# A linear-attention block with an MLP behind it on one Trainium2 core: half-width matmul blocks gathered, and the loads of four batches put in another order

## The chip, the core and the metric

The kernel runs on one NeuronCore of a Trainium2 chip. Its engines are TensorE (matmul, PE in the profile, its weight loads PEld), VectorE (DVE), ScalarE (ACT), GpSimd (POOL) and SyncE (SP); SP and POOL are used here to issue DMAs. Each engine works through its own instructions in the order in which the program emits them. The metric is the device time of one execution in microseconds (us), lower is better; a measurement is the median of several executions.

## What is computed

```python
# q, k, v: 8 batches x 8 heads x 576 positions x 64
kv  = einsum('bhsd,bhse->bhde', k, v)          # 64 x 64 per head
out = einsum('bhsd,bhde->bhse', q, kv)
out = out / sqrt(mean(out*out, -1) + 1e-6) * g_norm
x   = out.transpose(0, 2, 1, 3).reshape(8, 576, 512)
xn  = (x - mean(x)) / sqrt(var(x) + 1e-6) * g_ln
y   = x + relu(xn @ w_ch1) @ w_ch2             # 512 -> 2048 -> 512
```

The result is float32, 8 x 576 x 512. Matmuls run in bfloat16.

## The kernel before

**Tiling.** Of the 576 positions of a batch, 512 make four main tiles of 128 rows, and 64 are left. The 64 rows of two batches make one remainder tile, so batches 1, 3, 5 and 7 each close one (called remainder 1, 3, 5, 7). Four remainder tiles form a ninth block, "rem", which the MLP handles last.

**Stages of a batch b.** (1) q, k and v are loaded by POOL's DMA queue, six transfers (`load`, two for each tensor), float32 in HBM to bfloat16, into one of two sets of buffers (b % 2). (2) `kv_of(b)`, L238 to L250: 40 matmuls with 128 rows and 64 columns of weights (128*64 in the profile), pairs of which go to the lower and the upper half of the output partitions; then two ScalarE copies into `kv_pack`. (3) `turn_q_dma(b)`, L201 to L207: VectorE copies q into another order (L203), then SyncE issues a DMA that transposes it (L205) into `qt`. (4) For each tile a `plan_tile`, L371 to L396, with four steps: `first` makes o = q kv on TensorE (L271; a main tile has 4 matmuls of 128*128, a remainder tile 8 of 128*64), its square on ScalarE (L277) and the sum over each head on VectorE (L298); `second` makes the root (ScalarE L308, VectorE L315) and the normed x (VectorE L303, L322, L326, L332); `third` the variance (ScalarE L340); `fourth` the transpose of the normed rows, for batches 2 and up by a DMA on SyncE's queue (L352), into `xT_blk`. The o of a tile sits in one of two PSUM buffers from `first` to `second`. (5) The MLP: `mm1` (L413, ReLU on ScalarE L416) and `mm2` (L429), whose result VectorE combines with x (`finish`, L434) and SyncE stores by two DMAs (L447, L448). "Tile (3,0)" is tile 0 of batch 3.

**What sets the order.** The MLP's matmuls of all batches run one batch after the other. They are cut into ticks: a tick is four or eight matmuls of L413, or four of L429, and every batch has 32 ticks, 16 of `mm1` and 16 of `mm2`; batch b's begin at tick 32 b. An agenda, filled by hand with `at(slot, function)`, holds all other work: at the start of a tick its functions are emitted, sorted by their fractional slot, and each engine receives its part of them in that order. `finish` of a tile is emitted behind the tile's last L429, before the next tick. So the work of batches 2 to 7 up to `xT_blk` lies between the MLP matmuls of earlier batches. In this order, before: `kv_of(3)` at tick 56 and its q at 56.7, remainder 1 at 62 (second step at 64, turn at 69), main tiles of batch 3 at 66, 71, 76, 81, remainder 3 at 82, `kv_of(4)` at 84 and its q at 84.7, main tiles of batch 4 from 96; `kv_of(5)` at 115; remainder 5 at 146, `kv_of(6)` at 147, `kv_of(7)` at 179, remainder 7 at 210.

**Loads.** `load_batch` first copies one element on POOL for each of its arguments (a gate, L98): POOL's queue goes on only when what that element belongs to has arrived. Loads of batch b are gated by the transposed q of batch b-1, those of batch 4 also by the last transpose of batch 2's `xT_blk`. They are issued k, v, q at ticks 47 (batch 3), 68, 100, 132 and 164.

Of the kernel before, what the change touches and what calls it, by code (L numbers as in the profile page):

```python
# [14 lines left out]
def kernel(  # L15
# [11 lines left out]
    nc = tc.nc  # L27
    f32 = mybir.dt.float32
# [5 lines left out]
    B, H, S, D = q.shape  # L34
# [3 lines left out]
    nK = Dm // 128  # L38
    nDe = Dh // 128
    HP = H // 2  # L40
# [3 lines left out]
    J, JJ, JP = 4, 5, 9  # L44
    S_LO = 64 * JJ
    EPS = 1e-6
    NB = 2
# [8 lines left out]
    ps_m = ctx.enter_context(tc.psum_pool(name="ps_m", bufs=1))  # L56
# [15 lines left out]
    q_in = [consts.tile([128, H, JJ, D], bf16, name=f"q_in{i}") for i in range(NB)]  # L72
    k_in = [consts.tile([128, H, JJ, D], bf16, name=f"k_in{i}") for i in range(NB)]
    v_in = [consts.tile([128, H, JJ, D], bf16, name=f"v_in{i}") for i in range(NB)]
    kv_g = consts.tile([128, HP, 128], bf16)
    kv_pack = [consts.tile([128, HP, 128], bf16, name=f"kv_pack{i}") for i in range(4)]
# [9 lines left out]
    def lo(t, b, h0=0, h1=H):  # L86
        return t[b, h0:h1, :S_LO, :].rearrange("h (p j) d -> p h j d", j=JJ)

    def up(t, b, h0=0, h1=H):
        return t[b, h0:h1, S_LO:, :].rearrange("h (p j) d -> p h j d", j=J)  # L90

    def load(dst, t, b, h0=0, h1=H):
        nc.gpsimd.dma_start(dst[:64, h0:h1], lo(t, b, h0, h1))
        nc.gpsimd.dma_start(dst[64:, h0:h1, :J], up(t, b, h0, h1))

    def load_batch(b, *after):
        for element in after:
            nc.gpsimd.tensor_copy(gate, element)  # L98
        load(k_in[b % NB], k, b)
        load(v_in[b % NB], v, b)  # L100
        load(q_in[b % NB], q, b)

    def load_w1(c):
        n = Dh // 4
# [60 lines left out]
    qts, held, blks, rstds, m1s, q_ps = {}, {}, {}, {}, {}, {}  # L165
# [35 lines left out]
    def turn_q_dma(b):  # L201
        q_p = kv_in.tile([128, JJ, H, D], bf16, tag="qp", bufs=2)
        nc.vector.tensor_copy(q_p.rearrange("p j h d -> p h j d"), q_in[b % NB])  # L203
        q_t = qt_pool.tile([128, JJ, HP, 128], bf16, tag="qt", name="qt")
        nc.sync.dma_start_transpose(  # L205
            q_t.rearrange("p j hp t -> p (j hp) t"), q_p.rearrange("p j h d -> p (j h d)"))
        qts[b] = q_t  # L207
# [28 lines left out]
            nc.vector.tensor_mul(kv_g[D:, self.hps, D:], self.odd[D:], g[D:])  # L236
            del self.even, self.odd

    def kv_of(b):
        kv_ps = ps_m.tile([128, HP, D], f32, tag="misc", name="kv_ps")  # L240
        kvp = held[b] = kv_pack[b % 4]
        for hp in range(HP):
            for j in range(JJ):
                for hh in range(2):
                    h = 2 * hp + hh
                    nc.tensor.matmul(kv_ps[hh * D:hh * D + D, hp, :],  # L246
                                     lhsT=k_in[b % NB][:, h, j, :], rhs=v_in[b % NB][:, h, j, :],
                                     start=(j == 0), stop=(j == JJ - 1))
        nc.scalar.copy(kvp[:D, :, :D], kv_ps[:D])  # L249
        nc.scalar.copy(kvp[D:, :, D:], kv_ps[D:])  # L250

    def new_block(n, bufs):
        x_blk = xpool.tile([128, 4, Dm], f32, tag=f"x{n}", bufs=bufs, name="x_blk")
        st_blk = xpool.tile([128, 3, 4], f32, tag=f"st{n}", bufs=bufs, name="st_blk")
        xT_blk = xpool.tile([128, nK, 512], bf16, tag=f"xT{n}", bufs=bufs, name="xT_blk")
        return x_blk, st_blk, xT_blk
# [98 lines left out]
    def main_tile(b, j, pool=None, tag="ops"):  # L355
        q_t, kvp = qts[b], held[b]
        if b not in blks:
            blks[b] = new_block("main", 3)
        return Tile([(slice(0, 128), lambda hp: q_t[:, j, hp, :], kvp)], blks[b], j, pool, tag)

    def rem_tile(b):
        mms = []
        for half, bb in enumerate((b - 1, b)):
            qt, kp = qts.pop(bb), held.pop(bb)
            mms.append((slice(half * 64, (half + 1) * 64),
                        lambda hp, qt=qt: qt[:, J, hp, :64], kp))
        if "rem" not in blks:
            blks["rem"] = new_block("rem", 1)
        return Tile(mms, blks["rem"], b // 2)

    def plan_tile(s, make, turn_at, on_pe):  # L371
        box = []

        def first():
            t = make()
            box.append(t)
            t.o()
            t.sq()
            t.red()

        def second():
            t = box[0]
            t.y()
            t.x()
            t.xc()

        def third():
            box[0].var()

        def fourth():  # L390
            box[0].turn(on_pe)

        at(s, first)
        at(s + 2, second)
        at(s + 6, third)
        at(turn_at, fourth)  # L396

    def m1_of(b):
# [20 lines left out]
    def rstd_of(b):  # L419
        rstd = work.tile([128, 4], f32, tag="rstd", bufs=3, name="rstd")  # L420
        nc.scalar.activation(rstd, blks[b][1][:, 2, :], func=AF.Sqrt, scale=1.0 / Dm, bias=eps_sb)  # L421
        nc.vector.reciprocal(rstd, rstd)  # L422
        rstds[b] = rstd
# [45 lines left out]
    def at(slot, fn):  # L469
        agenda.setdefault(int(slot), []).append((slot, fn))  # L470
# [119 lines left out]
    def next_loads():  # L590
        nc.gpsimd.memset(k_in[0][64:, :, J], 0.0)
        nc.gpsimd.memset(v_in[0][64:, :, J], 0.0)
        load_batch(2)

    at(1, before_1)
    at(2, before_2)
    at(5, lambda: t[2].turn(True))
    at(5.1, before_5)
    at(9.5, next_loads)
    at(11, lambda: t[3].turn(True))  # L600
    for i in range(4):
# [17 lines left out]
    at(14.5, q_start)  # L619
    at(19, q_turns)  # L620
    at(22, lambda: kv_of(1))
    for j, s, tn in ((0, 24, 30), (1, 27, 34), (2, 31, 38), (3, 35, 42)):
        plan_tile(s, lambda j=j: main_tile(1, j), tn, True)
    at(46, lambda: rstd_of(1))

    at(36, lambda: kv_of(2))
    at(36.9, lambda: turn_q_dma(2))
    for j, s, tn in ((0, 45, 51), (1, 49, 55), (2, 53, 61), (3, 57.5, 64)):
        plan_tile(s, lambda j=j: main_tile(2, j), tn, False)
    plan_tile(62, lambda: rem_tile(1), 69, False)  # L630
    at(78, lambda: rstd_of(2))

    for b in range(3, B):
        s = 32 * b
        at(47 if b == 3 else s - 60,
           lambda b=b: load_batch(b, qts[b - 1][:1, J, HP - 1, 127:],
                                  *([blks[2][2][:1, nK - 1, 511:]] if b == 4 else [])))
        d = -41 if b == 3 else -45
        at(s + d + (1 if b < 5 else 0), lambda b=b: kv_of(b))
        at(s + d + 1.7, lambda b=b: turn_q_dma(b))  # L640
        for j in range(J):
            o = s + d + (11 if b == 3 else 13) + 5 * j
            plan_tile(o, lambda b=b, j=j: main_tile(b, j), o + 6, False)
        if b % 2:
            plan_tile(s - 14, lambda b=b: rem_tile(b), s - 8, False)
        at(s + 14, lambda b=b: rstd_of(b))
    at(32 * B + 14, lambda: rstd_of("rem"))


# [56 lines left out]
```

## Time and profile before

| | us |
|---|---|
| median of 5 executions | 290.61 (290.37 to 291.26) |
| the profiled execution | 290.71 |
| span in its profile, first to last instruction | 288.9 |
| TensorE busy | 281.5 |
| VectorE busy | 149.8 |
| ScalarE busy | 153.3 |
| POOL busy | 40.9 |
| L429, 560 matmuls of 128x512 | 125.5 |
| L413, all forms, 1024 | 131.6 |
| L246 (kv), 280 matmuls | 5.8 |
| L271 (o tiles), 156 matmuls | 13.7 |

TensorE's clock was granted at 0.999 of full speed. How to read the rows that follow in the prediction: a row of the timeline gives the start (us from the span's start), the length, engine, source line, operation, output<-inputs, weight tile as rows*columns, shape, and the number of instructions of one kind merged into the row; in brackets stands idle time before it, and what ended it. Matmuls overlap: the length of one runs to its modelled end and is longer than the distance to the next start, so the prediction works with distances between starts. For DMA issues the profile gives the time from issue to landing.

### The profile page before, as it was taken

What the parts mean: (1) busy time and instruction counts of PE and PEld (TensorE: products, weight loads), DVE (VectorE), ACT (ScalarE), POOL (GpSimd) and SP (SyncE); (2) the same over time, 40 slices, a digit from 0 to 9 for tenths busy, and PEclk for the clock granted to TensorE, in tenths of its full rate; (3) what the DMA queues carried; (4) which work ended last, traced back from release to release, by engine and by line L of the source; (5) the groups of instructions that cost most, each with busy time, mean ns of one, the idle gap of its engine ahead of it and who ended that gap; (6) DMA issues with size and microseconds to landing.
All of it is one profiled execution on the core that took longest, in us unless ns stands there. A gap on an engine that the chain in (4) does not pass through costs nothing.

```text
span 288.9 us, 5753 instructions
## 1 busy us (share of the span) xinstructions
PE 281.5 (97%) x2295; PEld 158.0 (55%) x2295; DVE 149.8 (52%) x331; ACT 153.3 (53%) x333; POOL 40.9 (14%) x69
## 2 busy tenths in 40 slices
PE   8889999999999999999999999999999999999994
PEld 3579746995479644444444444444444444444444
DVE  5774119938897783764376935762578200220022
ACT  3577844985379733872288318921893066016400
POOL 8522510041005004100500032000000000000000
PEclk9999999999999999999999999999999999999999
DMA  7999999879786969997995189947202410230033
GB/s 214 199 206 204 201 188 195 209 113 196 139 171 101 194 108 158 201 154 126 153 217 74 39 150 224 151 84 150 56 18 63 102 36 0 47 81 19 0 73 75
DMA packets 67546, 36.76 MB, mean 127 GB/s; under 512 B 35516, under 2 KB 62524, under 8 KB 67520
## 3 DMA queue, kind: packets, MB, share of 16 engines
q0 software_dynamic: 28528, 17.76, 44.8%
q1 hardware_dynamic: 38480, 17.91, 30.8%
q10 hardware_dynamic: 512, 0.72, 0.8%
q8 instruction: 18, 0.29, 0.4%
q14 instruction: 8, 0.07, 0.1%
HBM read 36.71 MB, written 9.44 MB: 160 GB/s over the span
## 4 chain that ended last, share of the span: by engine, by line
PE 84%; DVE 5%; DMA 5%; ACT 2%; issue 1%; SPq 1%; DVEq 0%; POOLq 0%
PE p L413 41%; PE p L429 37%; DMA v_in<-in_v_dram 2%; PE o_ps L271 2%; DMA qt<-q_p 2%; PE kv_ps L246 2%; DMA xT_blk<-xc 1%; DVE ss L298 1%; ACT m L416 1%; DVE x_blk L322 1%; DVE y L303 1%; DVE o_sb L434 1%; ACT rms L308 1%; SPq L205 1%; DVE x_blk L289 0%
## 5 line engine op out<-in xcount | busy, mean ns | idle before, releaser
L413 PE MATMUL p<-xT_blk,w_sb 128*128 128x128 bf16 (+2 forms) x1024 | 131.6, 286 | 0.7 <-DMA xT_blk<-xc 0.3
L429 PE MATMUL p<-w_sb,m 128*128 128x512 bf16 (+2 forms) x608 | 129.1, 368 | 0.0
L416 ACT ACTIVATE m<-p 128x512 bf16<-128x512 f32 x144 | 85.2, 596 | 43.0 <-PE p L413 40.5
L413 PEld LDWEIGHTS <-w_sb 128*128 128x128 bf16 x1024 | 78.7, 98 | 44.9 <-issue 1.6
L429 PEld LDWEIGHTS <-m 128*128 128x128 bf16 x608 | 56.9, 98 | 62.0
L434 DVE SCALAR_TENSOR_TENSOR o_sb<-p,rstd,x_blk 128x512 f32<-128x512 f32 (+2 forms) x38 | 27.3, 720 | 52.2 <-PE p L429 46.6
L277 ACT ACTIVATE sq<-o_ps 128x512 f32<-128x512 f32 x35 | 20.9, 596 | 41.7 <-PE o_ps L271 41.7
L298 DVE TENSOR_REDUCE ss<-sq 128x8 f32<-128x512 f32 x35 | 23.7, 678 | 13.1 <-ACT sq L277 13.0
L340 ACT ACTIVATE dev<-x_blk,st_blk 128x512 f32<-128x512 f32 x36 | 25.7, 714 | 6.2 <-DVE st_blk L326 6.1
L332 DVE SCALAR_TENSOR_TENSOR xc<-x_blk,st_blk,g_ln_sb 128x512 bf16<-128x512 f32 x34 | 25.6, 752 | 1.2
L303 DVE TENSOR_TENSOR y<-o_ps,inv 128x512 f32<-128x512 f32 x33 | 22.8, 692 | 3.4 <-PE p L413 0.5
L322 DVE SCALAR_TENSOR_TENSOR x_blk<-y,g_norm_sb 128x512 f32<-128x512 f32 x33 | 22.8, 692 | 1.1
L315 DVE RECIPROCAL inv<-rms 128x8 f32<-128x8 f32 x36 | 7.2, 201 | 23.1 <-ACT rms L308 23.1
L422 DVE RECIPROCAL rstd<-rstd 128x4 f32<-128x4 f32 x9 | 1.6, 175 | 31.1 <-ACT rstd L421 31.0
L308 ACT ACTIVATE rms<-ss,eps_sb 128x8 f32<-128x8 f32 x36 | 10.7, 296 | 11.6 <-DVE ss L298 11.5
L98 POOL COPY gate<-qt 1x1 bf16<-1x1 bf16 x5 | 0.9, 177 | 106.3 <-DMA qt<-q_p 106.3
L271 PEld LDWEIGHTS <-qt 128*128 128x128 bf16 (+1 forms) x156 | 10.2, 100 | 8.1 <-issue 1.7
L271 PE MATMUL o_ps<-kv_pack,qt 128*128 128x128 bf16 (+1 forms) x156 | 13.7, 220 | 0.1
L198 PE MATMUL p<-fill_sb 128*128 128x512 bf16 x27 | 8.5, 468 | 1.2 <-DVE eps_sb L137 1.2
L340 ACT ACTIVATION_READ_ACCUMULATOR dev<-x_blk,st_blk 128x1 f32 x36 | 6.8, 189 | 0.0
L249 ACT CAST kv_pack<-kv_ps 64x256 bf16<-64x256 f32 x7 | 2.6, 366 | 7.9 <-PE kv_ps L246 7.9
L246 PEld LDWEIGHTS <-k_in 128*64 128x64 bf16 x280 | 5.0, 112 | 2.9 <-issue 2.8
(80 smaller groups left out, 110.6 us busy)
## 6 DMA issues: line engine op xcount, KB each, us to landing
out_dram<-o_sb SPq DMA_DIRECT2D x70, 128.0 KB, 2.5
w_sb<-in_moe_w_ch_dram POOLq DMA_DIRECT2D x8, 512.0 KB, 15.3
q_in<-in_q_dram POOLq DMA_DIRECT2D x7, 320.0 KB, 12.4
k_in<-in_k_dram POOLq DMA_DIRECT2D x7, 320.0 KB, 6.2
v_in<-in_v_dram POOLq DMA_DIRECT2D x7, 320.0 KB, 9.0
q_in<-in_q_dram POOLq DMA_DIRECT2D x8, 256.0 KB, 12.6
k_in<-in_k_dram POOLq DMA_DIRECT2D x7, 256.0 KB, 7.2
v_in<-in_v_dram POOLq DMA_DIRECT2D x7, 256.0 KB, 9.9
```

What stands on the lines that cost most here:

```text
L271: nc.tensor.matmul(flat[rows, hp * 128:(hp + 1) * 128], lhsT=lhsT_of(hp), rhs=kvp[:, hp, :], start=True, stop=True)
L277: nc.scalar.activation(self.sq_t, self.o_ps, func=AF.Square)
L298: nc.vector.tensor_reduce(self.ss, self.sq_t, axis=AX.X, op=ALU.add)
L303: nc.vector.tensor_mul(self.y_t, self.o_ps, self.inv().to_broadcast([128, H, D]))
L308: nc.scalar.activation(self.r, self.ss, func=AF.Sqrt, scale=1.0 / D, bias=eps_sb)
L322: nc.vector.scalar_tensor_tensor(x_blk[:, ts].rearrange("p (h d) -> p h d", h=H), in0=self.y_t, scalar=1.0, in1=g_norm_sb.to_broadcast([12 ...
L332: nc.vector.scalar_tensor_tensor(self.xc_t, in0=x_blk[:, self.ts], scalar=st[:, 1, self.ts:self.ts + 1], in1=g_ln_sb, op0=ALU.add, op1=ALU ...
L340: nc.scalar.activation(dev, x_blk[:, ts], func=AF.Square, bias=st[:, 1, ts:ts + 1], accum_out=st[:, 2, ts:ts + 1])
L413: nc.tensor.matmul(p1[:, i, :], lhsT=w1_sb[:, kk, de * 128:(de + 1) * 128], rhs=blk[2][:, kk, sl], start=(kk == 0), stop=(kk == nK - 1))
L416: nc.scalar.activation(m1[:, de0:de0 + per, sl], p1, func=AF.Relu)
L429: nc.tensor.matmul(p2[:, c0:c1], lhsT=m1s[b][:, de, ts * 128:(ts + 1) * 128], rhs=w2_sb[:, de, c0:c1], start=(de == 0), stop=(de == nDe - 1))
L434: nc.vector.scalar_tensor_tensor(o_sb[:, c0:c1], in0=p2[:, c0:c1], scalar=rstds[b][:, ts:ts + 1], in1=blks[b][0][:, ts, c0:c1], op0=ALU.mu ...
```

## The change

`kv_of` takes one or more batches, computes them in one PSUM tile and copies them afterwards. Remainder tiles 1, 3 and 5 are emitted directly behind a kv block: remainder 1 behind kv 3 at tick 56.1 (its second step stays at 64, its turn at 69), remainder 3 behind kv 4 at 87.1 (kv 4 moves from 84 to 87, the second step is at 90, the turn at 96), remainder 5 behind kv 6 and kv 7, which are computed together at tick 152 (second step 154, turn 160). Remainder 7 and kv 5 stay. Main tiles of batch 3 stand at 66, 70.5, 75 and 79.5, those of batch 4 at 97, 101.75, 106.5 and 111.25; q of batch 4 is turned at 85.6. The loads of batch 4 are in the order q, k, v. Those of batch 6 are q, k, v, and k and v of batch 7 follow them at tick 132; q of batch 7 comes alone at 164. The gates are the same, but for k and v of batch 7, which are now behind the gate of batch 6.

```diff
-    def load_batch(b, *after):
+    def load_batches(what, *after):
         for element in after:
             nc.gpsimd.tensor_copy(gate, element)
-        load(k_in[b % NB], k, b)
-        load(v_in[b % NB], v, b)
-        load(q_in[b % NB], q, b)
+        tensors = {"k": (k_in, k), "v": (v_in, v), "q": (q_in, q)}
+        for name, b in what:
+            dst, src = tensors[name]
+            load(dst[b % NB], src, b)
...
-    def kv_of(b):
-        kv_ps = ps_m.tile([128, HP, D], f32, tag="misc", name="kv_ps")
-        kvp = held[b] = kv_pack[b % 4]
...
+    def kv_of(*bs):
+        kv_ps = ps_m.tile([128, len(bs), HP, D], f32, tag="misc", name="kv_ps")
+        for i, b in enumerate(bs):
+            for hp in range(HP):
+                for j in range(JJ):
+                    for hh in range(2):
+                        h = 2 * hp + hh
+                        nc.tensor.matmul(
+                            kv_ps[hh * D:hh * D + D, i, hp, :], lhsT=k_in[b % NB][:, h, j, :],
+                            rhs=v_in[b % NB][:, h, j, :], start=(j == 0), stop=(j == JJ - 1))
+        for i, b in enumerate(bs):
+            kvp = held[b] = kv_pack[b % 4]
+            nc.scalar.copy(kvp[:D, :, :D], kv_ps[:D, i])
+            nc.scalar.copy(kvp[D:, :, D:], kv_ps[D:, i])
...
-    def plan_tile(s, make, turn_at, on_pe):
+    def plan_tile(s, make, turn_at, on_pe, x_at=None):
...
-        at(s + 2, second)
-        at(s + 6, third)
+        at(x_at or s + 2, second)
+        at((x_at or s + 2) + 4, third)
...
-    plan_tile(62, lambda: rem_tile(1), 69, False)
...
-    for b in range(3, B):
-        s = 32 * b
-        at(47 if b == 3 else s - 60,
-           lambda b=b: load_batch(b, qts[b - 1][:1, J, HP - 1, 127:],
-                                  *([blks[2][2][:1, nK - 1, 511:]] if b == 4 else [])))
-        d = -41 if b == 3 else -45
-        at(s + d + (1 if b < 5 else 0), lambda b=b: kv_of(b))
-        at(s + d + 1.7, lambda b=b: turn_q_dma(b))
+    def turned_q(b):
+        return qts[b][:1, J, HP - 1, 127:]
+    at(47, lambda: load_batches((("k", 3), ("v", 3), ("q", 3)), turned_q(2)))
+    at(68, lambda: load_batches((("q", 4), ("k", 4), ("v", 4)),
+                                turned_q(3), blks[2][2][:1, nK - 1, 511:]))
+    at(100, lambda: load_batches((("k", 5), ("v", 5), ("q", 5)), turned_q(4)))
+    at(132, lambda: load_batches((("q", 6), ("k", 6), ("v", 6), ("k", 7), ("v", 7)),
+                                 turned_q(5)))
+    at(164, lambda: load_batches((("q", 7),), turned_q(6)))
+    at(115, lambda: kv_of(5))
+    for s, bs, rem, x_at, tn in ((56, (3,), 1, 64, 69), (87, (4,), 3, 90, 96),
+                                 (152, (6, 7), 5, 154, 160)):
+        at(s, lambda bs=bs: kv_of(*bs))
+        plan_tile(s + .1, lambda rem=rem: rem_tile(rem), tn, False, x_at)
+    plan_tile(210, lambda: rem_tile(7), 216, False)
+    for b, at_q, at_o, step in ((3, 56.7, 66, 4.5), (4, 85.6, 97, 4.75),
+                                *((b, 32 * b - 43.3, 32 * b - 32, 5) for b in range(5, B))):
+        at(at_q, lambda b=b: turn_q_dma(b))
         for j in range(J):
-            o = s + d + (11 if b == 3 else 13) + 5 * j
+            o = at_o + step * j
             plan_tile(o, lambda b=b, j=j: main_tile(b, j), o + 6, False)
-        if b % 2:
-            plan_tile(s - 14, lambda b=b: rem_tile(b), s - 8, False)
-        at(s + 14, lambda b=b: rstd_of(b))
+        at(32 * b + 14, lambda b=b: rstd_of(b))
```

More of the change, by code (lines that the diff above doesn't have):

```diff
@@ L237, in times_g @@
             del self.even, self.odd
-    def kv_of(b):
-        kv_ps = ps_m.tile([128, HP, D], f32, tag="misc", name="kv_ps")
-        kvp = held[b] = kv_pack[b % 4]
[L242 to L250, printed above, removed]
+    def kv_of(*bs):
[12 more added lines that the diff above has]
+            nc.scalar.copy(kvp[D:, :, D:], kv_ps[D:, i])
     def new_block(n, bufs):
@@ L592, in next_loads @@
         nc.gpsimd.memset(v_in[0][64:, :, J], 0.0)
-        load_batch(2)
+        load_batches((("k", 2), ("v", 2), ("q", 2)))
     at(1, before_1)
```

## The prediction

> **What bounds the kernel now.** I read the page first, then TensorE's row in the timeline (its waits list says nearly nothing), then VectorE, SyncE's queue and the POOL queue over 72 to 112 us.
>
> ```profile
> span 288.9 us, 5753 instructions
> PE 281.5 (97%) x2295; PEld 158.0 (55%) x2295; DVE 149.8 (52%) x331; ACT 153.3 (53%) x333; POOL 40.9 (14%) x69
> PE 84%; DVE 5%; DMA 5%; ACT 2%; issue 1%; SPq 1%; DVEq 0%; POOLq 0%
> ```
>
> TensorE has work in 97% of the span and is 84% of the chain that ended last. From 18 us on, a change is worth what it takes from TensorE's row: the pauses around the small-tile blocks, and the few stalls. TensorE's timeline around batch 5's blocks:
>
> ```profile
> 156.23 1.89 PE L429 MATMUL p<-w_sb,m 128*128 128x512 bf16 x8
> 158.05 0.41 PE L271 MATMUL o_ps<-kv_pack,qt 128*64 128x128 bf16 x8
> 158.40 1.04 PE L429 MATMUL p<-w_sb,m 128*128 128x512 bf16 x4
> 159.37 0.82 PE L246 MATMUL kv_ps<-v_in,k_in 128*64 128x64 bf16 x40
> 160.12 5.14 PE L429 MATMUL p<-w_sb,m 128*128 128x512 bf16 x23
> ```
>
> L429's pitch is 0.216 us (52 from 130.29 to 141.53). Eight from 156.23 end at 157.96; the remainder tile (128*64, half-width) starts at 158.05, and the next L429 at 158.40: 0.45 us with the 0.01 that the first L429 loses. Its work is 4 pairs that run side by side at about 0.055: 0.22. So 0.23 us is entry and exit. The kv block occupies 159.27 to 160.13, 0.86 us; its pairs have a pitch of 0.032 (19 pitches between its first and last start), 20 pairs make 0.63, and 0.23 is left again. An ordinary o tile (128*128) between L413s costs only its 0.22. **Price of one excursion into half-width tiling: 0.23 us**; there are eleven (kv 1 to 7, remainders 1, 3, 5, 7).
>
> The stalls: VectorE and SyncE bring q of batches 3 and 4 late.
>
> ```profile
> 81.24 1.91 PE L413 MATMUL p<-xT_blk,w_sb 128*128 128x256 bf16 x16
> 83.20 0.40 PE L271 MATMUL o_ps<-kv_pack,qt 128*128 128x128 bf16 x4
> ...
> 101.08 10.53 PE L429 MATMUL p<-w_sb,m 128*128 128x512 bf16 x48
> 111.69 0.40 PE L271 MATMUL o_ps<-kv_pack,qt 128*128 128x128 bf16 x4
> 112.37 4.48 PE L413 MATMUL p<-xT_blk,w_sb 128*128 128x512 bf16 x20 [0.29 <-DMA xT_blk<-xc]
> ```
>
> L413's 256-wide pitch is 0.109 (40 from 83.44 to 87.80), so 16 from 81.24 end at 82.99: tile (3,0) waited 0.21 for q 3's transpose (landed 83.16). 48 L429 from 101.08 end at 111.46: tile (4,0) waited 0.23 for q 4. Its four matmuls end at 111.91; L413 starts at 112.37, 0.46 late, for xT of tile (3,3), whose transpose stands behind q 4's on SyncE's queue.
>
> **Part 1, excursions.** kv 3 with remainder 1, kv 4 with remainder 3, and kv 6, kv 7 and remainder 5 become three blocks instead of seven: eleven become seven. Four times 0.23 is 0.92 less. That kv and remainder matmuls need no pause between each other no trace of before shows; both are 128*64. Bounds: all 0.92, or 0.23 only (kv 6 to kv 7, the same form). I take 0.92, since the rows give the same price to both forms.
>
> A rule puts this higher: the Trainium skill, "TensorE: Matmul & The Clock Gate", Single matmul latency, gives a lone matmul a fixed part of about 166 ns beyond its streaming at full clock. Two such drains would make an excursion 0.33 by estimate, and the sum 1.3 instead of 0.92; the rows above say 0.23, and they decide.
>
> **Part 2, q of batch 3 (worse).** Remainder 1's o, Square and reduction move from tick 62 to 56.1, ahead of the copy q_p at 56.7. VectorE runs without idle there:
>
> ```profile
> 76.20 0.74 DVE L434 SCALAR_TENSOR_TENSOR o_sb<-p,rstd,x_blk 128x512 f32<-128x512 f32 x1
> 76.86 0.82 DVE L203 COPY q_p<-q_in 128x2560 bf16<-128x2560 bf16 x1
> 77.60 0.68 DVE L298 TENSOR_REDUCE ss<-sq 128x8 f32<-128x512 f32 x1
> ```
>
> The added reduction (pitch 0.60) puts q_p at 77.46 to 78.28. SyncE's queue was busy with stores until 78.08 and began q 3's transpose at 78.18, so only 0.16 of the 0.60 reaches it: 78.34, landing 4.98 later at 83.32, tile (3,0) at 83.36. TensorE arrives there 0.23 earlier, at 82.76, and waits 0.60 instead of 0.21. So at this point the new kernel is 0.16 behind, the first excursion's gain already spent. ScalarE's added Square ends about 75.1, before its reader's turn. The o buffers cost nothing: tile (2,3) needs the one that y of (2,2) frees at 74.58, and TensorE comes at 74.76; the remainder's buffer is held to tick 64, and tile (3,0) can take the other.
>
> The same 0.60 goes down VectorE and SyncE: stores of batch 1 (82.04) and xT of (2,2) and (2,3) (83.19, 85.81) issue 0.60 later. xT of (2,3) landed about 88.42 (the gate below starts on it at 88.48), then 89.02; L413 needs it at tick 72, which TensorE now reaches at 83.36 + two o tiles of 0.22 + six ticks of 0.873 (eight L413) = 89.04. I put 0.05 there, about the gate's distance from the landing; a late transpose makes it 0.3.
>
> **Part 3, loads of batch 4.** They start when that xT has landed.
>
> ```profile
> 88.48 0.18 POOL L98 COPY gate<-xT_blk 1x1 bf16<-1x1 bf16 x1 [5.03 <-DMA xT_blk<-xc]
> 89.67 0.68 POOL L93 DMA_DIRECT2D k_in<-in_k_dram  x1 [1.00 <-PE p L413]
> ```
>
> The listing of DMA issues, asked for each one's stretch, gives landings at 94.9, 96.6 (k), 98.3, 100.0 (v), 101.9 and 103.1 (q): the last 13.4 after the first issue. The order q, k, v gives q these first places and v the last. The first issue comes 1.19 after the gate's start here, but 0.48 to 0.52 after it in batches 3, 5, 6 and 7; the gate at 89.08 therefore gives 89.6 to 90.3. I take 89.67, the time of before and next to what those four rows give, and v at 103.1 plus 0.3, because the store of batch 2's first tile moves from 103.31 to about 101.8 (VectorE no longer has remainder 3's chain before it) and meets the last load: 103.4. Bounds for the last landing from the other batches: 13.2 after the first issue (batch 3) and 15.6 (batch 6), 102.9 to 105.9.
>
> The 1.00 us has a page: the Trainium skill, "SBUF — State Buffer", SBUF: two separate sides, says that VectorE and GpSimd lock a shared port pair against each other, so that POOL cannot write descriptors meanwhile. VectorE's xc ran from 88.86 to 89.61 here. If that was the cause, the issue stays at 89.67 although the gate is later; without the rule it could be 90.3 and the sum 0.6 higher. No run here isolates it.
>
> TensorE reaches kv 4 (tick 87) so: 83.36, plus 12.91 (before: 83.20 to 96.11), plus 0.22 for tile (3,3), now before tick 80, plus 28 times 0.216 = 6.05: 102.54, with the 0.05 above 102.59. v lands 103.4, so **kv 4 waits about 0.85**; bounds 0.3 and 3.3, and nothing if the issue comes half a microsecond earlier. Queued behind it on TensorE is everything. This is the term that I am least sure of.
>
> In return q 4 lands at 96.6, its copy stands at tick 85.6 without remainder 3's chain ahead (about 101.7 instead of 105.75), and xT of (3,3) precedes it on SyncE: both waits at 111 to 112 go, 0.23 + 0.46 = 0.69. What is late next there, q 4's transpose, lands about 109, some 3 us early.
>
> **Part 4, batches 6 and 7.** Ten loads instead of six follow the gate, whose time moves with TensorE. Six took 15.6 from the first issue. Four more are 1.18 MB; at 196 GB/s (the rate of the stretch 95 to 98 us) 6.0, with a transpose's share some 6.6: 22.2. Tick 152 was at 164.46; without remainder 5 (0.45) and kv 6 (0.86) it is at 163.15, 24.0 after the old first issue at 139.12. Slack 1.8, so I cost it at nothing. The far end is batch 5's pace (six in 18.3, with three tiles' stores among them) for all ten: 30.5, a wait of 6.5; the stores lie in batch 6's 15.6 already, so this end is left in the tenth above the range. kv 7 leaves tick 179, q 7 alone follows later, and nothing waits for it.
>
> **The sum**, against the profiled run's 290.71 (span 288.9 plus 1.8 around it): excursions -0.92, q 3's wait +0.39, xT +0.05, kv 4's wait +0.85, old waits -0.69: -0.32, that is 290.4. The median shown is 0.10 below that run, so **290.3**. About 0.2% (0.6 us) is what a measurement tells from no change.
>
> **Rivals.**
> - *v of batch 4 lands in time* (wait under 0.5): -0.7 to -1.2, 289.4 to 289.9. For it: the six loads' last landings spread by microseconds, and an issue soon after the gate suffices. Against: 13.4 and the tick's place. 0.38.
> - *My sum*: wait 0.5 to 1.7, 289.9 to 291.1, centre 290.3. 0.43.
> - *Slower: v of batch 4 lands over 1.75 late at kv 4.* With batch 6's 15.6 after 89.67 it lands at 105.3, the wait is 2.7 and the time 292.1; it decides from a landing at 104.4. For it: stores and transposes share the engines; against: only one store is due before 103. 0.12.
> - *The blocks do not join* (a pause stays between kv and remainder): 0.69 of the gain goes, 291.0; with a longer wait 291.4. 0.07.
>
> Faster by over 0.2%: 0.38 and the lower edge of my sum, 0.41. Slower: 0.12, some of the last, 0.16. The rest 0.43. The range leaves out a tenth at either end: 289.4 to 291.3.
>
> **What would show it.** TensorE's row should have seven half-width blocks with one pause of 0.1 before and after each; tile (3,0) about 0.6 late at 83.4; a gap of 0.3 to 1.7 before the joined kv 4, ended by the load of v; no gap at 111 to 112; kv 6 and 7 without one. I am wrong if kv 4 waits nothing or above 1.7, if batch 7's v is late, or if the joined blocks keep inner pauses.

## The result, and the profile after

The changed kernel took 292.34 us (median of 27 executions, 290.96 to 295.87), the kernel before 290.67 in the same comparison (48 executions, 290.35 to 292.44): a ratio of 1.0063 with a 95% interval of 1.0049 to 1.0077. The ratio is one of means, without the longest run of the changed kernel (295.87), which is over 1.5% above its fastest; the medians alone give 1.0057. It is slower by 0.6%, and 292.34 lies above the range given. (Of the loads, those of three batches changed places, 4, 6 and 7; batches 3 and 5 keep their order.) The profiled execution took 291.98, 1.27 more than the one of before. Of its 28 executions, the profiled one among them, 11 have a mean granted TensorE clock of 0.987 to 0.994 and took 293.0 to 295.9 us; the other 17 have 0.997 to 1.0 and lie between 290.96 and 292.51 (median 291.73). A mean clock lower by 0.006 is 1.7 us lost, what 3.4 us at half clock take (e4 below shows such a stretch); none of the 11 was profiled, so that they had one, or two at 0.987, is inferred.

The page of the changed kernel, the rows that answer to the first ones of before. Lines stand three lower now (L247 is kv, L274 the o tiles, L416 and L432 the MLP, L355 xT's transpose, L450 and L451 the stores):

```profile
span 290.1 us, 5756 instructions
PE 280.1 (97%) x2295; PEld 158.0 (54%) x2295; DVE 149.7 (52%) x331; ACT 153.1 (53%) x333; POOL 41.4 (14%) x69
PE 79%; DMA 8%; DVE 7%; ACT 3%; issue 2%; POOL 1%; DVEq 0%; POOLq 0%
```

TensorE is busy 1.4 us less (280.1 for 281.5), and the span is 1.2 us longer. The chain says where to look: DMA's share rose from 5% to 8%. TensorE's timeline:

```profile
83.17 0.40 PE L274 MATMUL o_ps<-kv_pack,qt 128*128 128x128 bf16 x4 [0.37 <-DMA qt<-q_p]
...
96.33 6.21 PE L432 MATMUL p<-w_sb,m 128*128 128x512 bf16 x28
104.96 0.82 PE L247 MATMUL kv_ps<-v_in,k_in 128*64 128x64 bf16 x40 [2.43 <-DMA v_in<-in_v_dram]
105.59 0.42 PE L274 MATMUL o_ps<-kv_pack,qt 128*64 128x128 bf16 x8
105.94 7.94 PE L432 MATMUL p<-w_sb,m 128*128 128x512 bf16 x36
...
114.58 0.39 PE L274 MATMUL o_ps<-kv_pack,qt 128*128 128x128 bf16 x4
...
157.80 7.07 PE L432 MATMUL p<-w_sb,m 128*128 128x512 bf16 x32
164.80 1.46 PE L247 MATMUL kv_ps<-v_in,k_in 128*64 128x64 bf16 x80
166.09 0.39 PE L274 MATMUL o_ps<-kv_pack,qt 128*64 128x128 bf16 x8
```

The 28 matmuls from 96.33 end at 102.37 (the last starts at 102.15, and the pitch is 0.216); kv 4 starts at 104.96. So TensorE stands still for 2.59 us, until v of batch 4 has landed at 104.82. Remainder 3 follows kv 4 after 0.63, the 20 pairs at 0.032, with no pause between; so do kv 6, kv 7 and remainder 5 at 164.80. Tile (4,0) at 114.58 waits for nothing, but it also comes 2.9 later than before; e1 below shows the same where it comes at 112.21. What POOL does ahead of those loads:

```profile
88.95 0.67 POOL L98 COPY gate<-xT_blk 1x1 bf16<-1x1 bf16 x1 [5.53 <-DMA xT_blk<-xc]
90.14 0.68 POOL L93 DMA_DIRECT2D q_in<-in_q_dram  x1 [0.51 <-DVE xc L335]
```

The gate starts 0.47 later than before (88.48), and the first load is issued 0.47 later (89.67): 1.19 after the gate in both kernels, although the copy itself now took 0.67 instead of 0.18. The last load lands 14.68 after that first issue, instead of 13.43.

The account of the profiled execution: four excursions less -0.92, tile (3,0) waits 0.53 instead of 0.21, +0.32, kv 4 waits 2.59, the two waits at 111 to 112 are gone, -0.69: +1.30, of 1.27 measured. (About 0.1 of the 2.59 is the entry into kv 4's block, which the price of an excursion holds too.)

### The profile page after: what moved, and what is told of

Read it like the earlier page. It is cut to its first block, busy times and chain, and to the rows that moved or that the text cites. A ratio compares the mean times of both kernels' runs of the same rounds, so it can differ in the third digit from the quotient of the medians.

```text
span 290.1 us, 5756 instructions
## 1 busy us (share of the span) xinstructions
PE 280.1 (97%) x2295; PEld 158.0 (54%) x2295; DVE 149.7 (52%) x331; ACT 153.1 (53%) x333; POOL 41.4 (14%) x69
## 4 chain that ended last, share of the span: by engine, by line
PE 79%; DMA 8%; DVE 7%; ACT 3%; issue 2%; POOL 1%; DVEq 0%; POOLq 0%
PE p L416 37%; PE p L432 36%; DMA v_in<-in_v_dram 6%; PE o_ps L274 2%; DMA qt<-q_p 2%; PE kv_ps L247 2%; DVE x_blk L325 1%; DVE y L306 1%; ACT m L419 1%; DVE ss L301 1%; DVE o_sb L437 1%; ACT rms L311 1%; DVE xc L335 1%; DVE x_blk L292 0%; DVE xc L550 0%
## 5 line engine op out<-in xcount | busy, mean ns | idle before, releaser
L416 PE MATMUL p<-xT_blk,w_sb 128*128 128x128 bf16 (+2 forms) x1024 | 132.0, 286 | 0.4
L432 PE MATMUL p<-w_sb,m 128*128 128x512 bf16 (+2 forms) x608 | 128.2, 368 | 0.0
L419 ACT ACTIVATE m<-p 128x512 bf16<-128x512 f32 x144 | 85.1, 596 | 45.8 <-PE p L416 43.5
L416 PEld LDWEIGHTS <-w_sb 128*128 128x128 bf16 x1024 | 78.5, 98 | 44.6 <-issue 1.1
L432 PEld LDWEIGHTS <-m 128*128 128x128 bf16 x608 | 57.3, 98 | 62.9
L274 PE MATMUL o_ps<-kv_pack,qt 128*128 128x128 bf16 (+1 forms) x156 | 13.6, 220 | 0.4 <-DMA qt<-q_p 0.4
L274 PEld LDWEIGHTS <-qt 128*128 128x128 bf16 (+1 forms) x156 | 10.3, 100 | 6.6 <-DMA qt<-q_p 0.6
L252 ACT CAST kv_pack<-kv_ps 64x256 bf16<-64x256 f32 x7 | 2.6, 366 | 12.5 <-PE kv_ps L247 12.5
L247 PE MATMUL kv_ps<-v_in,k_in 128*64 128x64 bf16 x280 | 5.6, 197 | 2.5 <-DMA v_in<-in_v_dram 2.4
L247 PEld LDWEIGHTS <-k_in 128*64 128x64 bf16 x280 | 5.0, 112 | 4.9 <-issue 4.8
```

The source lines that it names most:

```text
L247: nc.tensor.matmul(kv_ps[hh * D:hh * D + D, i, hp, :], lhsT=k_in[b % NB][:, h, j, :], rhs=v_in[b % NB][:, h, j, :], start=(j == 0), stop=( ...
L274: nc.tensor.matmul(flat[rows, hp * 128:(hp + 1) * 128], lhsT=lhsT_of(hp), rhs=kvp[:, hp, :], start=True, stop=True)
L416: nc.tensor.matmul(p1[:, i, :], lhsT=w1_sb[:, kk, de * 128:(de + 1) * 128], rhs=blk[2][:, kk, sl], start=(kk == 0), stop=(kk == nK - 1))
L419: nc.scalar.activation(m1[:, de0:de0 + per, sl], p1, func=AF.Relu)
L432: nc.tensor.matmul(p2[:, c0:c1], lhsT=m1s[b][:, de, ts * 128:(ts + 1) * 128], rhs=w2_sb[:, de, c0:c1], start=(de == 0), stop=(de == nDe - 1))
```

## The experiments

My theory after the result: the change loses only by kv 4's wait for v, which it put last in the loads and pulled no later than tick 87. Rival: some other wait or price in the blocks eats the gain, and kv 4's wait would come back elsewhere.

**e1: kv 4 and remainder 3 six ticks later.**

```diff
-    for s, bs, rem, x_at, tn in ((56, (3,), 1, 64, 69), (87, (4,), 3, 90, 96),
+    for s, bs, rem, x_at, tn in ((56, (3,), 1, 64, 69), (93, (4,), 3, 95, 100),
```

> The changed kernel with one thing moved: kv 4 and remainder 3 from tick 87 to tick 93 (second step of the remainder at 95, its turn at 100). Theory (v of batch 4, now last in its queue, comes late and TensorE waits for it at kv 4: 2.59 us in the profile of the changed kernel): tick 93 is 6 times 0.864 = 5.2 us later, so the wait is gone and all else stays. Left are the excursions (-0.92), q of batch 3 (+0.32 by the profile of after) and the old waits at 111 to 112 us (-0.69): about 289.4, 1.3 below before, and the spread of the runs (291.0 to 295.9 in the changed kernel) shrinks to that of before (about 1 us). Rival (the joined half-width blocks, or the ten loads of batches 6 and 7, cost the time in the runs that were not profiled): the time stays above 290.7 and the spread stays wide.

Measured: 289.64 us (289.39 to 289.89), ratio to before 0.997 [0.9959, 0.9981]. v lands at 104.59, nearly as late as in the changed kernel, but kv 4 now comes at 107.77 and waits for nothing, nor does tile (4,0), by these rows of TensorE's timeline (no brackets):

```profile
107.77 0.82 PE L247 MATMUL kv_ps<-v_in,k_in 128*64 128x64 bf16 x40
112.21 0.39 PE L274 MATMUL o_ps<-kv_pack,qt 128*128 128x128 bf16 x4
```

**e2: the loads of batch 4 in the order k, v, q.**

```diff
-    at(68, lambda: load_batches((("q", 4), ("k", 4), ("v", 4)),
+    at(68, lambda: load_batches((("k", 4), ("v", 4), ("q", 4)),
```

> The changed kernel with the loads of batch 4 in the order of before (k, v, q); kv 4 stays at tick 87. Theory (the order makes v late): k and v land where q and k land in the profile of after (by about 101.3), kv 4 is reached at about 102.4 without a wait; q lands about 104.8, its copy holds VectorE up from 101.8 to 104.9, its transpose lands about 111 and tile (4,0) is reached about 112: no wait there or a small one. About 289.4 to 289.8. Rival (the loads as a whole are too late, the order only moves the wait): the wait returns at tile (4,0) and behind it, as 0.7 us or more, and the time is 290.1 or above.

Measured: 289.64 us (289.34 to 290.71), ratio 0.997 [0.9961, 0.998]. TensorE's timeline of this kernel (in this execution everything stands some 0.9 us later from the first stage on):

```profile
97.63 5.99 PE L432 MATMUL p<-w_sb,m 128*128 128x512 bf16 x27
103.55 0.82 PE L247 MATMUL kv_ps<-v_in,k_in 128*64 128x64 bf16 x40
```

No bracket stands behind kv 4: v had landed at 102.54. q, now last, landed at 105.90, and tile (4,0) did not wait for it either. Two different edits that only take away kv 4's wait give the same 289.64: the rest of the change is worth 0.3%, and the one wait costs more than that.

**e4: kv 4 three ticks earlier than in the change.** Does a longer wait cost its length, or more?

```diff
-    for s, bs, rem, x_at, tn in ((56, (3,), 1, 64, 69), (87, (4,), 3, 90, 96),
+    for s, bs, rem, x_at, tn in ((56, (3,), 1, 64, 69), (84, (4,), 3, 90, 96),
```

> The changed kernel with kv 4 and remainder 3 three ticks earlier, at 84, where kv 4 stood before; the order of loads stays q, k, v. Theory (TensorE waits until v lands, and the wait costs its length): 3 times 0.864 = 2.6 us more waiting, 5.2 in all, and about 294.9. Rival (a wait of more than some 3 us also lowers TensorE's granted clock, as the lower mean clock of the longest runs of the changed kernel, 0.991 to 0.994, hints): up to 2 us more, 296 to 297, and a stretch at half clock behind the wait in the profile.

Measured: 296.9 us (296.27 to 297.74), 4.6 above the changed kernel for three ticks of 0.86. The view by stretches (start:end, its length, busy time of PE, PEld, DVE, ACT and POOL, granted clock, DMA share, GB/s) has both halves of it:

```profile
99.90:105.40 5.50, 0.24 (x2) 0.00 (x1) 2.14 (x5) 0.00 (x0) 0.00 (x0) 0.95 1.29 210
105.40:108.30 2.90, 2.54 (x51) 1.93 (x53) 0.16 (x1) 1.52 (x4) 0.00 (x0) 0.51 0.14 21
```

TensorE waits 5.5 us, and in the next stretch its clock is granted at 0.51. By the clock's records in the trace the half clock lasts 3.41 us, from 104.84 to 108.25, and costs up to half of that, 1.7. In the changed kernel the mean clock of 11 of 28 executions fits such a window. The Trainium skill, "TensorE: Matmul & The Clock Gate", What's actually happening, says that the clock is halved after an idle window of about 3.4 us, and that the windows run on their own grid. The length agrees (3.41), and so does the grid: within one execution the changes of the clock lie whole multiples of 3.41 us apart (25 in e3 and e7, 29 in e4, 33 in e6). The idle time does not: waits of 2.3 to 2.5 us were enough in e3 and e7 below, and 2.4 was not in the profiled execution of the changed kernel. Laid on the grid these cases part. The clock halved where TensorE stood still (between the last start plus its pitch and the next start) for 2.49 us (e7), 2.70 (e3) or all 3.41 (e4, e6) of one interval of the grid. It did not where the grid cut a wait in two: the changed kernel's 2.59 us into 1.76 and 0.82, e11's 2.38 into 0.56 and 1.82. So a wait of some 2.5 us costs its length, or 1.7 us more, by where it falls.

**e5: the price of an excursion.** e1 with kv 4 apart from remainder 3, and kv 6, kv 7 and remainder 5 apart.

```diff
-    for s, bs, rem, x_at, tn in ((56, (3,), 1, 64, 69), (87, (4,), 3, 90, 96),
-                                 (152, (6, 7), 5, 154, 160)):
-        at(s, lambda bs=bs: kv_of(*bs))
-        plan_tile(s + .1, lambda rem=rem: rem_tile(rem), tn, False, x_at)
+    for s, b in ((56, 3), (93, 4), (151, 6), (152, 7)):
+        at(s, lambda b=b: kv_of(b))
+    for s, rem, x_at, tn in ((56.1, 1, 64, 69), (94.1, 3, 96, 101), (153.1, 5, 155, 161)):
+        plan_tile(s, lambda rem=rem: rem_tile(rem), tn, False, x_at)
```

> kv 4 at tick 93 as in e1_kv4_at_93, but remainder 3 a tick behind kv 4 (94.1), kv 6 at 151, kv 7 at 152 and remainder 5 at 153.1: three more excursions into half-width tiling than e1_kv4_at_93 (289.64 us), nothing else. My theory: 0.23 us each, so 0.69 more: about 290.3 us, with a pause on both sides of every block in the timeline. Rival: an excursion's pause costs nothing when the blocks stand apart by a tick, since the stalls elsewhere take it up: 289.6 us, within 0.2 of e1.

Measured: 290.08 us (290.01 to 290.47), 0.44 above e1 (before took 290.5 beside both). The timelines of e1 and of e5 reach tick 144 at the same time, 155.44 and 155.43. The next o tile behind the blocks is this row of e1:

```profile
170.96 0.39 PE L274 MATMUL o_ps<-kv_pack,qt 128*128 128x128 bf16 x4
```

and this one of e5:

```profile
171.41 0.39 PE L274 MATMUL o_ps<-kv_pack,qt 128*128 128x128 bf16 x4
```

Two excursions more are 0.46, so 0.23 each, as the prediction had it. The third, at remainder 3, shows in the stretch from tick 80 to 96 (14.91 instead of 14.68 us), but e5's profiled execution stood 0.24 ahead of e1's already at 81 us, before any of the three (L416 begins at 80.80 and 81.04). That is why the spans of these two profiles differ by 0.5 and not 0.69; whether the medians have the same reason is not shown.

**e6: what makes v late.** The transposes of tiles (3,1) to (3,3) put behind kv 4.

```diff
-            plan_tile(o, lambda b=b, j=j: main_tile(b, j), o + 6, False)
+            plan_tile(o, lambda b=b, j=j: main_tile(b, j),
+                      88.2 if b == 3 and j else o + 6, False)
```

> The changed kernel with the transposes of tiles (3,1), (3,2) and (3,3) put off to tick 88.2, behind kv 4, so that none of them runs among the loads of batch 4 (90 to 105 us). The loads then share the DMA engines with q 4's transpose and the stores of batch 2 only. My theory: those transposes account for most of what v of batch 4 lands later (14.7 us behind the first issue instead of 13.4), so it lands 13.0 to 13.6 behind, TensorE's wait at kv 4 falls from 2.6 to between 1.2 and 1.6, and the time to 290.4 to 291.0 us. Rival: the queue of the loads itself sets the landing: 14.4 to 14.8 behind the first issue, wait 2.3 to 2.7, time as the changed kernel's, 291.5 to 292.5.

Measured: 299.17 us (298.66 to 299.84), ratio 1.0297 [1.028, 1.0314]. Both expectations missed the time, but the landing decides: v lands at 102.81, 12.47 after the first issue (the theory had 13.0 to 13.6, the rival 14.4 to 14.8), and kv 4 waits 0.2. The gain was given back later. The three transposes now met the loads of batch 5, the last of them landed at 119.56, and TensorE, which needed it at 111.7, waited 7.8 us at tick 96 by the view. Two windows of half clock (6.83 us, from 116.57) began within that wait and went on behind it. The DMA view from first issue to last landing of batch 4 (queue, packets, MB, share of the 16 engines), of the kernel before:

```profile
q0 software_dynamic: 3168, 1.77, 96.9%
q1 hardware_dynamic: 1636, 0.39, 20.0%
```

of the changed kernel:

```profile
q0 software_dynamic: 3168, 1.77, 92.4%
q1 hardware_dynamic: 2072, 0.71, 26.7%
```

and of e6:

```profile
q0 software_dynamic: 3168, 1.77, 104.4%
q1 hardware_dynamic: 573, 0.14, 5.9%
```

The loads (q0) are the same 1.77 MB. What SyncE's queue puts among them (q1, transposes and stores) is 0.14, 0.39 and 0.71 MB, and the last landing comes 12.47, 13.43 and 14.68 after the first issue. The count ends with the landing, so a later landing counts more bytes by itself; e6, where an edit took the bytes away, speaks for them as the cause. Other kernels stand in about the same order: e7 with 0.26 MB and 13.23, e3 0.31 and 12.91, e9 0.53 and 14.53, e4 0.73 and 14.96. The change moves tile (3,2)'s transpose from 98.61 to 97.55, so that it lands ahead of the last load (104.76) and not behind it (103.79 against 103.10), and the two stores of tile (2,0) from 103.3 to 101.95, so that they run beside the last load. Of the 0.32 MB that the changed kernel has more than before, 0.25 are packets of 2048 bytes, the stores. The fifth load landed 0.44 later behind the first issue than before (12.72 for 12.28), and the sixth 1.25. So the stores are probably the larger part; e6 moved only transposes, and the stores alone were not tried.

**e3 and e7: away with the wait at tile (3,0).** In e1, 0.54 us of waiting are left there. e3 copies q of batch 3 before remainder 1's reduction and puts tile (3,0) a tick later; e7 does the latter alone.

```diff
-    for b, at_q, at_o, step in ((3, 56.7, 66, 4.5), (4, 85.6, 97, 4.75),
+    for b, at_q, at_o, step in ((3, 56.05, 67, 4.25), (4, 85.6, 97, 4.75),     # e3
+    for b, at_q, at_o, step in ((3, 56.7, 67, 4.25), (4, 85.6, 97, 4.75),      # e7
```

> The changed kernel with kv 4 and remainder 3 at tick 93, and with the copy of q of batch 3 ahead of kv 3 and remainder 1 (56.05 instead of 56.7) and the main tiles of batch 3 at 67, 71.25, 75.5 and 79.75 instead of 66, 70.5, 75 and 79.5. Theory (the wait of 0.53 us at tile (3,0) is the reduction put ahead of that copy, and one tick more covers the rest): 0.5 below the kernel with only kv 4 moved, about 288.9. Rival (that wait is hidden behind later waits, or the later tiles of batch 3 make batch 3's xT late): no gain, 289.4 or above.

> e1_kv4_at_93 with tile (3,0) at tick 67 in place of 66 and the steps between the main tiles of batch 3 at 4.25, q of batch 3 where it was. This is the other half of e3_kv4_at_93_q3_first. Theory of the fetch: TensorE no longer waits 0.54 at tile (3,0), so the 16 KB packet on the instruction queue comes at about 88.3 us, just behind the packets of tile (2,3)'s transpose (87.5 to 88.3 in e1): no wait at tick 72, and 289.1 us. If the two meet after all, a wait of 1 to 2.5 us stands at tick 72, and the time is 290 to 293. Rival (the place 67 itself makes tile (2,3)'s xT late, whatever the fetch): the wait of 2.7 us stands there with the fetch at 88.3 or later, and 293 us.

Measured: e3 293.33 us (291.22 to 294.16), e7 293.0 (292.95 to 293.18), over 3 us slower than e1. My theory for e3 fell. Tile (3,0) no longer waits, but TensorE does at tick 72, for xT of tile (2,3), and at half clock afterwards. TensorE's timeline of e3:

```profile
87.28 1.04 PE L416 MATMUL p<-xT_blk,w_sb 128*128 128x256 bf16 x8
90.86 4.46 PE L416 MATMUL p<-xT_blk,w_sb 128*128 128x256 bf16 x24 [2.53 <-DMA xT_blk<-xc]
```

That transpose was issued at 86.13, 0.29 earlier than in e1, and landed at 90.81, 1.86 later. In the DMA view of 87.4 to 88.0 us of e3 stands a queue of another kind:

```profile
q1 hardware_dynamic: 448, 0.12, 113.6%
q8 instruction: 1, 0.02, 18.2%
```

One packet of 16 KB. Eighteen such packets come in each execution, and this one starts in all kernels when TensorE has begun 2216 to 2245 instructions, so it goes with TensorE's progress: it is most likely TensorE's own next block of instructions. It took 1.75 us here, and the transpose's packets of 256 and 4 bytes that started at about 88.0 lasted until 90.0. At 2.5 us from issue to landing, as in e1, the transpose would have landed at 88.7 in e3 and 88.5 in e7, still 0.5 after TensorE came to tick 72; the packet would be the other 2 us of the wait. Rival: the place of the tiles itself.

**e8 and e9: moving the packet, or moving the transpose.** e8 is e3 with 14 more matmuls in kv 2 (they are overwritten), so that the packet comes earlier. e9 is e7 with the transpose of (2,3) ahead of two stores on SyncE's queue, and remainder 1's reduction later, so that its rows are ready.

```diff
+        if bs == (2,):                                                         # e8
+            for _ in range(7):
+                for hh in range(2):
+                    nc.tensor.matmul(kv_ps[hh * D:hh * D + D, 0, 0, :], lhsT=k_in[0][:, hh, 0, :],
+                                     rhs=v_in[0][:, hh, 0, :], start=True, stop=True)
...
-    for j, s, tn in ((0, 45, 51), (1, 49, 55), (2, 53, 61), (3, 57.5, 64)):
+    for j, s, tn in ((0, 45, 51), (1, 49, 55), (2, 53, 61), (3, 57.5, 63)):    # e9, e10
...
-            t.red()
+            if x_at != 64:                                                     # e9, e10
+                t.red()
...
             t = box[0]
+            if x_at == 64:
+                t.red()
             t.y()
```

> e3_kv4_at_93_q3_first (293.33 us) with 14 more matmuls in kv 2, whose result is written over by the real ones: some 0.2 us more work, and 28 more instructions on TensorE ahead of tick 71, so that the 16 KB packet on the instruction queue should come about 1.5 us earlier, at 86 instead of 87.5 us, ahead of tile (2,3)'s transpose. Theory of the fetch: the wait at tick 72 falls from 2.7 to under 0.5 us, the half clock behind it goes, and the time is 289.1 to 289.6 us although there is more work. Rival (the order of the SyncE or VectorE work makes xT late): wait 2.7 as before, 293.3 to 293.6 us.

> e7_place_67 (293.0 us) with the transpose of tile (2,3) on SyncE's queue ahead of the stores of tile (1,3) (tick 63 in place of 64), and remainder 1's reduction on VectorE moved behind, to its second step, so that (2,3)'s rows are ready in time. The transpose should then be issued at about 84.8 instead of 86.0 us and land at about 87.3, before the 16 KB packet on the instruction queue at 88.05. Theory of the fetch: no wait at tick 72, none at tile (3,0), so 0.5 less than e1_kv4_at_93 (289.64): 289.0 to 289.3 us, below all kernels so far. Rival (something else makes xT late whenever tile (3,0) does not wait): a wait of 1 to 2.5 us at tick 72 and 291 to 293 us.

Measured: e8 291.12 us (290.6 to 292.92), 2.2 faster than e3 with more work in it, but not the 289.1 to 289.6 expected: the packet came only 0.2 earlier, at 87.31, and the wait fell to 1.39; why it moved so little is not known. e9 289.20 us (289.12 to 289.85), ratio 0.9957 [0.9945, 0.997], as the theory had it and the fastest of all. Rows of e9's timeline (L419 is `mm1` here):

```profile
87.28 0.39 PE L274 MATMUL o_ps<-kv_pack,qt 128*128 128x128 bf16 x4
87.50 3.66 PE L419 MATMUL p<-xT_blk,w_sb 128*128 128x256 bf16 x32
```

Tick 72 runs through without a wait. All profiles that bear on it:

| | (2,3) issued | the packet starts, after that | landed, after that | wait at tick 72 |
|---|---|---|---|---|
| changed | 86.30 | 2.41 | 2.54 | none |
| e1 | 86.42 | 2.41 | 2.53 | none |
| e7 | 86.01 | 2.04 | 4.48 | 2.32 |
| e3 | 86.13 | 1.37 | 4.68 | 2.53 |
| e8 | 86.56 | 0.75 | 3.56 | 1.39 |
| e9 | 84.19 | 3.97 | 2.50 | none |

The transpose of (2,3) takes 2.5 us from issue to landing, and 3.6 to 4.7 where the packet starts 0.75 to 2.04 after its issue; at 2.41, just ahead of the landing, it does no harm. In the changed kernel and in e1 the packet meets the next transpose on the queue, remainder 1's (issued at 87.70 and 87.81): that one takes 3.9 and 3.5 us, and nothing waits for it there. The place of the tiles, the rival, is the same in e7 and e9. In e9 the transpose is also issued 1.8 earlier than in e7, so that even 2 us more would have cost only some 0.3 us: what points to the packet is the time to landing in the table, more than e9's result.

**e10, e11, e12: the earlier transpose in the changed kernel, and two second looks.** e10 is the changed kernel with e9's two edits; e11 is e10 once more, e12 the changed kernel once more.

> The changed kernel with the same earlier transpose of tile (2,3), kv 4 at tick 87 and q first as in the change. Theory (the first load follows the second gate by a constant 1.19 us, the gate follows xT of tile (2,3), and v lands 14.4 to 14.7 us behind the first load): landing of (2,3) 87.5 instead of 88.84, gate 87.6, first load 88.8, v 103.2 to 103.5, kv 4 waits 0.9 to 1.2 us instead of 2.6, no half clock; 290.4 to 290.9 us, and the runs lie close together. Rival (the transposes among the loads set v's landing, and they do not move): v lands at 104.8 as before, wait 2.4 to 2.6, 291.5 to 292.5 us.

> e10_early_turn_after once more, unchanged, for a second profile. Its twelve runs lay between 289.4 and 293.4 us, and the profiled one (291.29) was among the slower. Theory: the landing of v of batch 4 differs by 1 to 2 us between executions of one kernel, because the loads and three transposes meet on the same DMA engines; most executions have it at 102.3 to 103.0 us, kv 4 waits 0 to 0.9 us, and this run takes 289.4 to 290.0 us. Rival: the landing is 104.0 in every execution, and the runs differ elsewhere (clock, other waits): v at 103.9 to 104.2 whatever the run's time.

> The changed kernel once more, unchanged, for a second profile beside the one with v at 104.82 us and a wait of 2.6 us. Theory: v lands between 103.8 and 105.8, kv 4 waits for what lies beyond 102.4, and the time follows it: 291.0 us at 103.9, 292.0 at 104.8, and 1.7 us more on top where the wait is so long that the half clock follows. Rival (v lands in the same place in every execution): 104.7 to 104.9, a wait of 2.5 to 2.7, and a time that differs from 292.0 only through the clock.

Measured: e10 289.93 us (twelve runs, 289.4 to 293.43), ratio 0.9991 [0.9969, 1.0014]; e11 291.79, e12 292.18 (one run each). The first half of e10's theory held, 0.8 earlier than it had said: xT landed at 86.68, the gate started at 86.80, the first load was issued at 87.98, 1.18 later. The second half did not: v landed at 104.05, 16.07 after the issue, and in e11 at 104.61, 16.29 after it, with waits of 2.0 and 2.2 at kv 4. In e9, with loads issued at the same time, it landed 14.53 after. SyncE's queue put more among the loads here than in any other kernel, 0.75 and 0.77 MB, but hardly more than in e4 (0.73, and 14.96). e11 missed both its theory and its rival; e12 had v at 105.00, 0.18 later than the first profile of the changed kernel, and nearly the same wait, as its rival had it. So why e10's median is 2.4 below the changed kernel's, and why its runs spread, is not explained by what I have: no quick run of it was profiled, and the theory that the landing wanders by 1 to 2 us between runs is not shown. What is shown is that loads issued 2 us earlier landed only 0.2 to 0.8 earlier.

## Why the prediction was wrong

- **Excursions, -0.92: right.** Seven blocks, no pause inside them, 0.23 each (e5).
- **q of batch 3, +0.39: right in kind, 0.32 measured.** The order was as worked out, the copy behind the added reduction, but all of it came 0.1 to 0.2 earlier: the copy at 77.33 (77.46 predicted), the transpose at 78.18, landed 83.13 (78.34 and 83.32), the tile at 83.17 (83.36). The transpose was issued at 78.18 in both kernels, so none of the 0.16 that the sum passed on came.
- **xT at tick 72, +0.05: nothing in the changed kernel.** It landed at 88.84, 0.03 ahead of TensorE. But this landing has a cliff that the prediction did not see: where tile (3,0) does not wait, the 16 KB packet meets this transpose and makes it 2 us later (e3, e7).
- **kv 4's wait, +0.85: this step failed.** It measured 2.59, and the 1.74 above the sum's 0.85 has three parts. First, "I take 89.67" for the first load: it came at 90.14, since the issue follows the second gate by a constant, 1.18 to 1.19 in all fourteen profiles, the 1.19 of before that the prediction showed among them; +0.47. Second, "v at 103.1 plus 0.3, because the store of batch 2's first tile moves": from the first issue to the landing the sum had 13.7, and 14.68 passed, since two stores and more of the transposes, 0.32 MB, came among the loads (e6 shows it for transposes, for the stores it is argued); +0.95. Third, TensorE was there at 102.37 and not at 102.59; +0.22. The last 0.10 lies between the landing and kv 4's start. Both ends of the landing, 102.9 and 105.9, held; I took a value near the lower one. The bounds named 13.2 (batch 3) and 15.6 (batch 6) from first issue to last landing; batches 5 and 7 of before had taken 18.3 and 16.2, so 13.7 was near the least of four.
- **The reasons for 89.67** do not hold. The four rows of 0.48 to 0.52 are of batches with one gate, and this one has two. The page named beside them does not fit either: the Trainium skill, "SBUF — State Buffer", SBUF: two separate sides, on the port pair that VectorE and GpSimd lock against each other. In e3, VectorE was idle from 89.96 on, by this row:

```profile
94.24 0.20 DVE L318 RECIPROCAL inv<-rms 128x8 f32<-128x8 f32 x1 [4.29 <-ACT rms L311]
```

and POOL still took 1.19 from gate to issue:

```profile
90.93 0.18 POOL L98 COPY gate<-xT_blk 1x1 bf16<-1x1 bf16 x1 [7.77 <-DMA xT_blk<-xc]
92.12 0.68 POOL L93 DMA_DIRECT2D q_in<-in_q_dram  x1 [1.01 <-issue]
```

What fills the 1.19 is not known; the batches with one gate take 0.48 to 0.52.

- **Old waits, -0.69: right** (e1, where tile (4,0) comes at 112.21 and waits for nothing), and batches 6 and 7 had a slack of 2.2 (1.8 predicted).
- **What no term had:** the half clock behind a long wait, 1.7 us where it came, by the mean clock in 11 of 28 executions. The median is 292.34 with these runs and 291.73 without, so the wait alone already puts the time above the range's 291.3.

The rival that came true is the slower one: v over 1.75 late, 292.1, from a landing at 104.4. It landed at 104.82. Its argument "for" was the one that counted (stores and transposes share the engines); the argument against it, "only one store is due before 103", left out that a tile's store is two DMAs of 128 KB, and the transposes. The landing it worked with, 15.6 after 89.67, was not the one that came, 14.68 after 90.14; that 292.1 is so near 292.34 is in part luck, for the median also holds runs at half clock.

## What to carry to other kernels

When a change puts a load last and its reader earlier, list every transfer that any queue will issue between the first issue and the last landing, in the new order, and add up the bytes: the loads share the DMA engines with all of them. A wait added where TensorE has none can cost more than its length: behind waits of 2.3 us and more (by the view) the half clock followed here, always or in part of the executions. And an edit that only makes TensorE faster can move a packet of the instruction queue onto a transfer that was just in time, so look at the tightest landings again after each gain.

## What the hardware showed that I had not expected

- Where one packet of 16 KB on the instruction queue, 1.0 to 1.8 us long, started 0.75 to 2.04 us after the issue of a DMA transpose, that transpose landed 1.0 to 2.2 us later than the usual 2.5 us (e3, e7, e8; remainder 1's in the changed kernel and e1). The packet alone was moved only in e8, by 0.2 us.
- A wait of 2.3 to 2.5 us on TensorE was followed by 3.41 us at a granted clock of 0.51 in some profiles (e3, e7) and not in others (changed, e12); those of 5.3 and 7.8 us were, and the mean clock of all nine executions of e4 and e6 is 0.991 or less. The clock changed on a grid of 3.41 us: 2.49 us of standstill within one interval were enough, 1.82 were not.
- From the last gate copy on POOL to the first load's issue, 1.18 to 1.19 us pass where two gates stand ahead of the load, whether the copy takes 0.18 or 0.71, and 0.48 to 0.52 where one does. That the second gate is the cause was not tried.
- Six loads of 1.77 MB in all (batch 4) land 12.5 to 15.0 us after the first issue, the later the more SyncE's queue has put among them (0.14 to 0.73 MB); in e10 and e11, which began 2 us earlier, 16.1 to 16.3 with 0.75 and 0.77 MB, and that stays open.
